# Scan attention and two feed-forward layers on one core: the second block's scores made as the first's are, an earlier place for the first block's inputs, and one PSUM bank given from the hidden products to attention

## The chip, the cores and the metric

The kernel runs on one core of one Trainium2 chip. The metric is device time of one execution in microseconds (us). The five engines of the core work on their own instruction streams and wait for each other by semaphores: TensorE (PE in the rows; its weight loads are PEld), VectorE (DVE), ScalarE (ACT), GpSimd (POOL) and SyncE (SP), which here issues every DMA. PSUM has eight banks; TensorE writes there, and VectorE and ScalarE read it.

## What is computed

First a chunked linear attention with decay over 4 batches, 8 heads, 768 positions, head size 32 and state size 16; then two feed-forward layers on the 3072 x 256 result, with 2048 hidden columns each.

```
for c in range(nc):                       # state carried from chunk to chunk
    cum = np.cumsum(log_a chunk)
    M = (Cc @ Bc.T) * exp(cum_i - cum_j) * causal
    y = M @ xc + (Cc @ state) * exp(cum)
    state = exp(sum) * state + sum_j exp(cum_last - cum_j) * Bc_j xc_j
x = y reshaped to 3072 x 256
x = elu(x @ moe_w_in) @ moe_w_out
out = mish(x @ moe2_w_in) @ moe2_w_out    # mish(h) = h * tanh(softplus(h))
```

## The kernel before

**Attention.** The kernel uses chunks of T = 96 positions. A tile is one batch at one chunk; tiles are numbered i = 4c + b, 32 in all, and the four tiles of one chunk are a block of 384 tokens. For each tile the scores (C times B, eight heads) come from TensorE into PSUM, VectorE multiplies them with the decay matrix `d` into `r` (`at_p`, L655, two products of four heads; `at_p0`, L643, four of two heads), TensorE multiplies `r` with x into `ys` (`at_y`, L677), computes the state for the next chunk (`at_st`, L709), and ScalarE and VectorE write `ys` as a high and a low part, `xyh` and `xyl` (L690, L696), the input of layer 1. `d` comes from a broadcast load of the cumulated logarithms, an addition (L536), a mask (L540) and an exponential (L545).

**Two ways to the scores.** C and B stand in memory with positions on partitions and must be transposed. Tiles in `TR0`, the first block, take the way of `at_tr0`: four fp32 transposes on TensorE into PSUM (`p_tr`, L603), one copy to SBUF (`f32t`, by ScalarE or VectorE), and eight fp32 matmuls with 16 rows each (`at_scores0`, L637), half of them per call, each half into two banks. All other tiles go through `three_parts`: C and B are split into three bf16 parts that are stacked (`stk`: two copies L506 and two L517 on ScalarE, two subtractions L511 and two L523 on VectorE or GpSimd), a DMA transpose turns the stack (L527), and eight bf16 matmuls give the scores (`at_scores`, L649), half of them per call and each half in one bank.

**Feed-forward.** A slot s is one group of 128 hidden columns of one block in one layer; 16 slots make a block of a layer, 256 slots in all, in the order of the list `order` (layer 1 of blocks 0 and 1, layer 2 of blocks 0 and 1, layer 1 of block 2, and then layer 1 and 2 in turn). TensorE makes h of a slot with six matmuls (L745 to L747: high times high, low and high parts), ScalarE and VectorE apply the activation (layer 1: L760, then L766 or L768, then L774 or L776, the last to read h; layer 2: L791 alone), split the result (`gh`, `gl`), and TensorE adds it up into `acc` some slots later (layer 1: L807 to L809; layer 2: L836 to L838; the first 16 slots do it in fp32 without a split, L812). Weights arrive in 512 KB pieces (`load_job`, L312) and each is rounded and split by `job_1` to `job_5`: L325 and L341 on VectorE, L334 on ScalarE, a copy L349 or L351, a subtraction L365 on VectorE or GpSimd.

**PSUM.** Pool `ph` (tag `h`) has HB = 4 banks: h, and the first block's scores and decay sums. Pool `pa` (tag `acc`) has 3. Pool `px` (tag `s`) has 1: transposes, the other blocks' scores and their `ys`.

**Order.** Every piece of work is a `step` with engine choices, an assumed cost and the steps that it needs. `Ring` makes a step that takes a buffer wait for those that free it. `run_steps` goes through an assumed time, gives each engine the most urgent step that is ready, and writes the instructions of each engine in that order; on the chip each engine runs its list in order. `in_turn` forces an order on some loads. No times of the chip go into it.

Of the kernel before, what the change touches and what calls it, by code (L numbers as in the profile page):

```python
# [7 lines left out]
F32 = mybir.dt.float32  # L8
# [9 lines left out]
def tile_chain(  # L18
# [13 lines left out]
    NB, H, S, D = x.shape  # L32
    N = Bm.shape[-1]
    T = 96
# [6 lines left out]
    NP = NF // FP  # L41
    LAG = 5
    N0 = NF
    TR0 = (0, 1, 2, 3)
    WB, GB, HB = 4, 3, 4

    const = ctx.enter_context(tc.tile_pool(name="const", bufs=1))
    wpool = ctx.enter_context(tc.tile_pool(name="wpool", bufs=1))
# [2 lines left out]
    gp = ctx.enter_context(tc.tile_pool(name="gp", bufs=GB))  # L51
    at = ctx.enter_context(tc.tile_pool(name="at", bufs=1))
    ph = ctx.enter_context(tc.tile_pool(name="ph", bufs=HB, space=bass.MemoryType.PSUM))
    pa = ctx.enter_context(tc.tile_pool(name="pa", bufs=3, space=bass.MemoryType.PSUM))
    px = ctx.enter_context(tc.tile_pool(name="px", bufs=1, space=bass.MemoryType.PSUM))
    dram = ctx.enter_context(tc.tile_pool(name="dram", bufs=1, space=bass.MemoryType.DRAM))

    ctx.enter_context(tc.manual_schedule())
# [5 lines left out]
    A, V, G, PE, DQ = "act", "dve", "pool", "pe", "sp"  # L64
# [9 lines left out]
    in_turn = []  # L74

    def step(opts, *deps, dl=1e9):
        steps.append((opts if isinstance(opts, list) else [opts], deps, dl))
        return len(steps) - 1
# [9 lines left out]
    class Ring:  # L88
# [5 lines left out]
        def take(self):  # L94
            self.free.append([])
            k = len(self.free) - 1
            return self.free[k], Need(self, k, self.free[k - self.n] if k >= self.n else [])

    class Need:
# [6 lines left out]
            return iter(self.free)  # L106

    rings = dict(
        w=Ring(WB), gh=Ring(GB), gl=Ring(GB), h=Ring(HB), acc=Ring(3), s=Ring(1), xy=Ring(3), x=Ring(5), bc=Ring(2),
        d=Ring(2), r=Ring(1), t=Ring(2), r1=Ring(1), bw=Ring(2), raw=Ring(2), o=Ring(3), stk=Ring(1),  # L110
    )

# [375 lines left out]
    d_t, bct, rr_t, bw_t, sp_t, s_t, ys_t, f32_t = {}, {}, {}, {}, {}, {}, {}, {}  # L488
# [109 lines left out]
    def at_tr0(i):  # L598
        p = tl["tr", i] = px.tile([112, 2, 2, T], F32, tag="s", name="p_tr")
        for z, src in enumerate((c_t[i], b_t[i])):  # L600
            for g in range(2):

                nc.tensor.transpose(  # L603
                    p[:, z, g, :], src.rearrange("p h n -> p (h n)")[:, N * g:N * g + 112], ident[0:T, 0:T]
                )

    def at_tr0_out(i, eng):
        t = f32_t[i] = gp.tile([112, 2, 2, T], F32, tag="g" + "hl"[i // 2], name="f32t")
        copy(eng, t, tl["tr", i])

    def at_diff0(i, g):
# [17 lines left out]

    def at_scores0(i, half):  # L630

        s = s_t[i, half] = [p.tile([T, 2, T], F32, tag=t, name="s") for p, t in ((ph, "h"), (pa, "acc"))]
        for g in range(2):
            for z in range(2):
                q = 32 * (2 * half + z)
                v = f32_t[i][q:q + N]
                nc.tensor.matmul(out=s[z][:, g, :], lhsT=v[:, 1, g, :], rhs=v[:, 0, g, :], start=True, stop=True)  # L637

    def at_p0(i, half):
        s, r = s_t.pop((i, half)), new_r(i)  # L640
        for z in range(2):
            hs = slice(4 * half + 2 * z, 4 * half + 2 * z + 2)
            nc.vector.tensor_tensor(out=r[0:T, hs, :], in0=s[z], in1=d_t[i][0:T, hs, :], op=ALU.mult)  # L643
# [83 lines left out]
    acc = {}  # L727
# [133 lines left out]
    def alt(f, *opts):  # L861

        return [(e, cost, lambda e=e: f(e)) for e, cost in opts]
# [4 lines left out]
    s_lc = [step((DQ, 0.48, lambda i=i: load_bc0(Cm, c_t, "xyh", i), 0.95)) for i in range(NB)]  # L868
    s_lb = [step((DQ, 0.48, lambda i=i: load_bc0(Bm, b_t, "xyl", i), 0.95)) for i in range(NB)]
# [34 lines left out]
    w_ready, LW = {}, []  # L904
    r_1, _ = take("raw")
    r_2, _ = take("raw")
# [20 lines left out]
    LX, YHI, YLO, SO, BW, xf, xy_f = {}, {}, {}, {}, {}, {}, {}  # L927
# [3 lines left out]
        LX[i] = step((DQ, 0.48, lambda i=i: load_x(i), 0.95), n)  # L931
    in_turn.append([s_la])
    for i in range(NB):
        in_turn[-1] += [s_lc[i], s_lb[i], LX[i]] + LW[i:i + 1]

    for key in [("x", 0), ("x", 1), ("y", 0), ("x", 2), ("y", 1), ("x", 3)]:
        xy_f[key] = take("xy")
# [5 lines left out]
    def three_parts(i, need):  # L943

        sf, sn = take("stk")
        rf, rn = take("r1")
        a1 = step((A, 0.82, lambda: at_split_1(i)), need, sn)
        a2 = step(alt(lambda e: at_split_2(i, e), (V, 0.40), (G, 0.45)), a1, rn)
        a3 = step((A, 0.62, lambda: at_split_3(i)), a2)
        a4 = step(alt(lambda e: at_split_4(i, e), (V, 0.40), (G, 0.45)), a3)  # L950
        tf, tn = take("t")
        a5 = step((DQ, 0.62, lambda: at_split_5(i), 2.0, True), a4, tn)
        lock.update((a2, a4))
        rf.append(a4)
        sf.append(a5)
        return a2, a5, tf

    def two_scores(i, a5, tf, ex, r_n, cold):
        pz = []
        for z in range(2):  # L960
            pf, pn = take("s")
            sc = step((PE, 0.4 if cold else 0.33, lambda z=z: at_scores(i, z)), a5, pn)
            pz.append(step((V, 0.47, lambda z=z: at_p(i, z)), sc, ex, r_n))
            pf.append(pz[-1])
            tf.append(sc)
        return pz

    for i in range(NB):
        cold = i in TR0
        if cold:  # L970
            tf, tn = take("s")
            tr = step((PE, 0.64, lambda i=i: at_tr0(i)), s_lc[i], s_lb[i], s_c2, tn)
# [4 lines left out]
        else:  # L977
            a2, a5, tf = three_parts(i, [s_lc[i], s_lb[i]])
            bc0_f.append(a2)
        if i == 0:  # L980
# [7 lines left out]
            d_f, _ = take("d")  # L988
        else:
            if i < 2:  # L990
                d_f, _ = take("d")
# [9 lines left out]
        ex = step((A, 0.78, lambda i=i: at_exp(i)), mk)  # L1001
        table[ex] = "exp"
        if i in (1, 2):
            r_f, r_n = (r_1, []) if i == 1 else (r_2, [])
        else:
            r_f, r_n = take("r")
        if cold:
            pz = []
            for z in range(2):
                hf, hn = take("h")  # L1010
                af, an = take("acc")
                sc = step((PE, 0.7, lambda i=i, z=z: at_scores0(i, z)), cp, hn, an)
# [4 lines left out]
        else:  # L1017
            pz = two_scores(i, a5, tf, ex, r_n, True)
# [23 lines left out]
    for i in range(NB, tiles):  # L1042
        c, b = divmod(i, NB)
        bcf, bcn = take("bc")
        lb = step((DQ, 0.96, lambda i=i: load_bc(i), 1.9), bcn)
        l96 = step((DQ, 1.44, lambda i=i: load_c96(i), 0.15), lb)
        d_f, d_n = take("d")
        lc = step((DQ, 0.48, lambda i=i: at_cumrow(i), 0.82), s_q4[c], d_n)
        a2, a5, tf = three_parts(i, lb)
        dd = []  # L1050
        for g in range(2):
            f = lambda e, i=i, g=g: at_diff(i, g * H // 2, (g + 1) * H // 2, e)
            dd.append(step(alt(f, (G, 1.0), (V, 0.47)), lc, s_q6))
            lock.add(dd[-1])
        mk = step((G, 0.95, lambda i=i: at_mask(i)), dd)
        ex = step((A, 0.78, lambda i=i: at_exp(i)), mk)
        table[ex] = "exp"
        cs = step((G, 0.95, lambda i=i: at_cs(i)), l96, lc, s_d5)
        r_f, r_n = take("r")
        rc = step((V, 0.56, lambda i=i: at_rc(i)), cs, r_n)  # L1060
        rc2 = step(alt(lambda e, i=i: at_rc2(i, e), (V, 0.27), (A, 0.41)), rc)
        lock.add(rc2)
        bcf += [a2, cs]
        if c + 1 < NCH:
            bf, bn = take("bw")
            b1 = step((G, 0.42, lambda i=i: at_bw_1(i)), lb, s_d3, bn)
            b2 = step((G, 0.42, lambda i=i: at_bw_2(i)), s_d7, b1)
            bcf.append(b1)
        pz = two_scores(i, a5, tf, ex, r_n, False)
        d_f += pz + [rc]  # L1070
        pf, pn = take("s")
        if c + 1 < NCH:
            y = step((PE, 0.76, lambda i=i: (at_y(i), at_st(i))), pz, rc, rc2, LX[i], pn, SO[i - NB], b1, b2)
            SO[i] = step((V, 0.34, lambda i=i: at_st_out(i)), y, LX[i + NB])
            pf.append(SO[i])
            bf.append(y)
        else:
            y = step((PE, 0.57, lambda i=i: at_y(i)), pz, rc, rc2, LX[i], pn, SO[i - NB])
        r_f.append(y)
        YHI[i] = step((A, 0.21, lambda i=i: at_y_hi(i)), y, xy_f["x", c][1])  # L1080
        YLO[i] = step((V, 0.27, lambda i=i: at_y_lo(i)), YHI[i])
        pf += [YHI[i], YLO[i]]
        xf[i].append(y)
# [3 lines left out]
    for s in range(len(order) * NF):  # L1087
        layer, c, f = at_slot(s)
        blk = s // NF
        if f == 0 and s:  # L1090
# [3 lines left out]
        h = HS[s] = step((PE, 1.95 if s < 2 else 1.04, lambda s=s: emit_h(s)), src, w_ready[f"i{layer}", f // FP], hn,  # L1094
                         HS.get(s - 1, []), dl=slot_time(s))
# [7 lines left out]
        if layer == 1:  # L1103
            e = step((A, 0.37, lambda s=s: elu_1(s)), h, wn)
            table[e] = "exp"
            e = step(alt(lambda e, s=s: elu_2(s, e), (V, 0.27), (A, 0.41)), e)
            lock.add(e)
            e = step((V, 0.47, lambda s=s: elu_3(s)), e)
        else:
            e = step((A, 0.37, lambda s=s: mish_1(s)), h, wn)  # L1110
# [3 lines left out]
        if split:  # L1114
            gf, gn = take("gh")
            lf, ln = take("gl")
            two = [(A, 0.41), (V, 0.27)]
            gh = step(alt(lambda e, s=s: split_hi(s, e), *(two if layer == 1 else two[::-1])), e, gn)
# [66 lines left out]
```

## Time and profile before

| what | us |
|---|---|
| median of 3 runs | 638.46 |
| lowest and highest | 637.58, 639.07 |
| the profiled execution | 640.66 |
| its span, first to last instruction | 638.9 |

The profiled execution lies 0.3% above the median. Of its 640.66 us the span is 638.9 us; the rest, 1.8 us, lies around it. The profile gives for each engine its busy time and, at each wait, what ended it. TensorE's busy time also holds stretches at the lower of its two clock levels.

### The profile page before, as it was taken

Reading aid. Unit: us, or ns where it says so; the run is one execution under the profiler, and the core shown is the slowest. Engines: PE = TensorE matmul, PEld = TensorE weight load, DVE = VectorE, ACT = ScalarE, POOL = GpSimd, SP = SyncE. Lnnn points to the kernel's source line nnn. Section 1 sums busy time; section 2 is a strip of 40 time slices with the busy share of each in tenths; the row PEclk is TensorE's granted clock in tenths of the full one; section 3 lists DMA queues with packets and bytes.
Section 4 is the critical chain, followed back from the end, with each engine's and each line's share of the span. In section 5 each row is a group of like instructions: output and inputs, shape, how many; then the busy total and the mean of one; then the engine's idle time right before and its main releaser. Section 6 shows DMA issues by size and latency. Waiting matters only on the chain.

```text
span 638.9 us, 12337 instructions
## 1 busy us (share of the span) xinstructions
PE 614.3 (96%) x4500; PEld 584.1 (91%) x4500; DVE 457.3 (72%) x937; ACT 402.7 (63%) x753; POOL 194.6 (30%) x259
## 2 busy tenths in 40 slices
PE   5897899998999999999999999999999999999996
PEld 4575679998999899999999999999999999999996
DVE  5688889977868887677675877668875777644443
ACT  5577888998956676548854687447855554442221
POOL 2456484453304672025600274013500210000000
PEclk9598999998999999999999999999999999999999
DMA  7789765446243552025510554024410220000000
GB/s 176 143 206 251 205 150 137 122 127 158 62 42 75 107 98 33 1 51 93 94 26 1 96 104 63 1 51 84 85 39 1 44 46 25 2 1 1 9 18 25
DMA packets 139933, 48.75 MB, mean 76 GB/s; under 512 B 122944, under 2 KB 128704, under 8 KB 139872
## 3 DMA queue, kind: packets, MB, share of 16 engines
q1 hardware_dynamic: 139872, 47.96, 35.3%
q8 instruction: 35, 0.57, 0.4%
q14 instruction: 26, 0.21, 0.1%
HBM read 32.31 MB, written 3.24 MB: 56 GB/s over the span
## 4 chain that ended last, share of the span: by engine, by line
PE 80%; DVE 7%; ACT 4%; DMA 2%; issue 2%; POOL 0%; DVEq 0%; POOLq 0%; ACTq 0%
PE h L745 13%; PE h L746 12%; PE h L747 12%; PE acc L836 7%; PE acc L838 7%; PE acc L837 7%; PE acc L807 5%; PE acc L809 5%; PE acc L808 5%; PE acc L812 3%; PE ys L709 2%; PE ys L677 2%; PE s L649 1%; DMA d<-cum_d 1%; DVE raw L341 1%
## 5 line engine op out<-in xcount | busy, mean ns | idle before, releaser
L745 PE MATMUL h<-xyh,wi 128*128 128x384 f32 x512 | 178.7, 349 | 1.7 <-ACT xyh L690 1.7
L746 PE MATMUL h<-xyl,wi 128*128 128x384 f32 x512 | 173.2, 338 | 0.1
L747 PE MATMUL h<-xyh,wi 128*128 128x384 f32 x512 | 172.8, 338 | 0.0
L787 DVE TENSOR_TENSOR gl<-w,gh 128x384 fp32r<-128x384 f32 x219 | 132.6, 609 | 17.9 <-ACT gh L349 9.0
L791 ACT ACTIVATE w<-h 128x384 f32<-128x384 f32 x128 | 61.7, 491 | 92.5 <-PE h L747 85.3
L836 PE MATMUL acc<-wo,gh 128*128 128x256 f32 x384 | 111.3, 290 | 0.0
L838 PE MATMUL acc<-wo,gl 128*128 128x256 f32 x384 | 108.5, 283 | 0.6 <-POOL gl L787 0.3
L837 PE MATMUL acc<-wo,gh 128*128 128x256 f32 x384 | 108.1, 282 | 0.0
L745 PEld LDWEIGHTS h<-xyh,wi 128*128 128x128 f32 x512 | 97.8, 191 | 4.8 <-ACT xyh L690 2.0
L746 PEld LDWEIGHTS h<-xyl,wi 128*128 128x128 f32 x512 | 97.8, 191 | 1.5 <-DVE xyl L696 0.5
L747 PEld LDWEIGHTS h<-xyh,wi 128*128 128x128 f32 x512 | 97.2, 190 | 0.2 <-DVE wi L365 0.2
L351 DVE CAST gh<-w 128x384 fp32r<-128x384 f32 x119 | 50.5, 426 | 59.5 <-PE acc L837 40.0
L760 ACT ACTIVATE w<-h 128x384 f32<-128x384 f32 x112 | 54.4, 488 | 49.7 <-PE h L747 45.2
L349 ACT ACTIVATE gh<-w 128x384 fp32r<-128x384 f32 x121 | 63.3, 523 | 31.1 <-PE acc L808 23.2
L807 PE MATMUL acc<-gh,wo 128*128 128x384 f32 x224 | 76.1, 340 | 1.1 <-DVE xyl L823 1.1
L808 PE MATMUL acc<-gh,wo 128*128 128x384 f32 x224 | 74.9, 335 | 0.0
L809 PE MATMUL acc<-gl,wo 128*128 128x384 f32 x224 | 74.9, 335 | 0.0
L838 PEld LDWEIGHTS acc<-wo,gl 128*128 128x128 f32 x384 | 72.9, 190 | 1.2 <-DVE gl L787 0.7
L836 PEld LDWEIGHTS acc<-wo,gh 128*128 128x128 f32 x384 | 72.5, 189 | 1.1
L837 PEld LDWEIGHTS acc<-wo,gh 128*128 128x128 f32 x384 | 72.7, 189 | 0.0
L768 DVE TENSOR_SCALAR w<-w 128x384 f32<-128x384 f32 x85 | 33.2, 392 | 40.2 <-ACT w L760 40.0
L536 POOL TENSOR_TENSOR d<-d,dk 96x384 f32<-96x384 f32 x39 | 35.9, 930 | 71.5 <-DMA d<-cum_d 60.5
(102 smaller groups left out, 961.7 us busy)
## 6 DMA issues: line engine op xcount, KB each, us to landing
d<-cum_d SPq DMA_DIRECT2D x31, 288.0 KB, 3.9
raw<-in_moe_w_in_dram SPq DMA_DIRECT2D x16, 512.0 KB, 5.3
raw<-in_moe_w_out_dram SPq DMA_DIRECT2D x16, 512.0 KB, 4.1
xs<-in_x_dram SPq DMA_DIRECT2D x32, 96.0 KB, 3.4
bc<-in_C_dram SPq DMA_DIRECT2D x32, 48.0 KB, 3.1
bc<-in_B_dram SPq DMA_DIRECT2D x32, 48.0 KB, 3.2
out_dram<-o SPq DMA_DIRECT2D x16, 96.0 KB, 1.8
bc<-bc SPq DMA_DIRECT2D x84, 16.0 KB, 1.8
```

Of the source, the lines that this page charges most:

```text
L349: nc.scalar.activation(out=out, in_=in_, func=AF.Copy)
L745: nc.tensor.matmul(out=h, lhsT=hi[:, k, fs], rhs=xh[:, k, :], start=(k == 0), stop=False)
L746: nc.tensor.matmul(out=h, lhsT=hi[:, k, fs], rhs=xl[:, k, :], start=False, stop=False)
L747: nc.tensor.matmul(out=h, lhsT=lo[:, k, fs], rhs=xh[:, k, :], start=False, stop=(k == 1))
L787: alu(eng).tensor_tensor(out=gl, in0=w, in1=gh.bitcast(F32), op=ALU.subtract)
L791: nc.scalar.activation(out=new_w(s), in_=st[s][0], func=AF.Mish)
L807: nc.tensor.matmul(out=y, lhsT=hi[:, f % FP, ds], rhs=gh, start=(f == 0), stop=False)
L808: nc.tensor.matmul(out=y, lhsT=lo[:, f % FP, ds], rhs=gh, start=False, stop=False)
L809: nc.tensor.matmul(out=y, lhsT=hi[:, f % FP, ds], rhs=gl, start=False, stop=(f == NF - 1))
L836: nc.tensor.matmul(out=y, lhsT=gh[:, ts], rhs=hi[:, f % FP, :], start=(f == 0), stop=False)
L837: nc.tensor.matmul(out=y, lhsT=gh[:, ts], rhs=lo[:, f % FP, :], start=False, stop=False)
L838: nc.tensor.matmul(out=y, lhsT=gl[:, ts], rhs=hi[:, f % FP, :], start=False, stop=(f == NF - 1))
```

## The change

Three edits. `TR0` becomes the first eight tiles, so that the second block (tiles 4 to 7) takes the transposing way as well; its `f32t` lies in the buffers that held the turned stack, and its scores take two `px` banks for each half. `HB` falls from 4 to 3 and `px` rises from 1 bank to 2, for the whole kernel. And the forced order of the first loads no longer has a weight load behind each tile's C, B and x: the first block's 12 loads come in a row, and the weights are free to be placed.

```
-    TR0 = (0, 1, 2, 3)
-    WB, GB, HB = 4, 3, 4
+    TR0 = range(2 * NB)
+    WB, GB, HB = 4, 3, 3
...
-    px = ctx.enter_context(tc.tile_pool(name="px", bufs=1, space=bass.MemoryType.PSUM))
+    px = ctx.enter_context(tc.tile_pool(name="px", bufs=2, space=bass.MemoryType.PSUM))
...
     def at_tr0_out(i, eng):
-        t = f32_t[i] = gp.tile([112, 2, 2, T], F32, tag="g" + "hl"[i // 2], name="f32t")
+        if i < NB:
+            t = f32_t[i] = gp.tile([112, 2, 2, T], F32, tag="g" + "hl"[i // 2], name="f32t")
+        else:
+            t = f32_t[i] = at.tile([112, 2, 2, T], F32, tag="t", name="f32t", bufs=2)
...
-        s = s_t[i, half] = [p.tile([T, 2, T], F32, tag=t, name="s") for p, t in ((ph, "h"), (pa, "acc"))]
+        banks = ((ph, "h"), (pa, "acc")) if i < NB else ((px, "s"), (px, "s"))
+        s = s_t[i, half] = [p.tile([T, 2, T], F32, tag=t, name="s") for p, t in banks]
...
-        in_turn[-1] += [s_lc[i], s_lb[i], LX[i]] + LW[i:i + 1]
+        in_turn[-1] += [s_lc[i], s_lb[i], LX[i]]
...
-        a2, a5, tf = three_parts(i, lb)
+        cold = i in TR0
+        if cold:
+            pf, pn = take("s")
+            tr = step((PE, 0.6, lambda i=i: at_tr0(i)), lb, pn)
+            tf, tn = take("t")
+            a2 = step(alt(lambda e, i=i: at_tr0_out(i, e), (A, 0.37), (V, 0.47)), tr, tn)
+            pf.append(a2)
+        else:
+            a2, a5, tf = three_parts(i, lb)
...
-        pz = two_scores(i, a5, tf, ex, r_n, False)
+        if cold:
+            pz = []
+            for z in range(2):
+                two = [take("s"), take("s")]
+                sc = step((PE, 0.65, lambda i=i, z=z: at_scores0(i, z)), a2, [n for _, n in two])
+                tf.append(sc)
+                pz.append(step((V, 0.61, lambda i=i, z=z: at_p0(i, z)), sc, ex, r_n))
+                for pf, _ in two:
+                    pf.append(pz[-1])
+        else:
+            pz = two_scores(i, a5, tf, ex, r_n, False)
```

The whole list is laid out anew, so the instructions of every engine stand elsewhere. Two places follow.

SyncE's queue from the fourth load of the program on, before the change; `bc_107` and `bc_113` are C and B of the first block, `xs` is x, `raw` a weight piece, and `d<-cum_d` the broadcast load of a tile's logarithms:

```order
L283 DMA xs<-in_x_dram 96x8x32
L312 DMA raw_118<-in_moe_w_in_dram 128x2x512
L434 DMA cum_d<-cum 16x2x96
L264 DMA bc_107<-in_C_dram 96x8x16
L264 DMA bc_113<-in_B_dram 96x8x16
L499 DMA d<-cum_d 96x768 x2
L283 DMA xs<-in_x_dram 96x8x32
L312 DMA raw_178<-in_moe_w_in_dram 128x2x512
```

And with the change, from the second tile's x on (the ninth load):

```order
L283 DMA xs<-in_x_dram 96x8x32
L264 DMA bc_107<-in_C_dram 96x8x16
L499 DMA d<-cum_d 96x768 x2
L264 DMA bc_113<-in_B_dram 96x8x16
L499 DMA d<-cum_d 96x768
L283 DMA xs<-in_x_dram 96x8x32
L264 DMA bc_107<-in_C_dram 96x8x16
L264 DMA bc_113<-in_B_dram 96x8x16
L312 DMA raw_237<-in_moe_w_in_dram 128x2x512
L283 DMA xs<-in_x_dram 96x8x32
L312 DMA raw_266<-in_moe_w_in_dram 128x2x512
```

The first weight piece moved from the 5th load to the 17th, behind C and B of all four tiles; the second stands two loads further down.

TensorE at the scores of tile 5 before the change, with buffer numbers: `s_676` and `s_692` are the two halves of the scores.

```order
L649 LDWEIGHTS t_522
L649 MATMUL s_676<-t_522 96x96
L649 LDWEIGHTS t_522
L649 MATMUL s_692<-t_522 96x96
L649 LDWEIGHTS t_522
L649 MATMUL s_692<-t_522 96x96
L649 LDWEIGHTS t_522
L649 MATMUL s_692<-t_522 96x96
L649 LDWEIGHTS t_522
L649 MATMUL s_692<-t_522 96x96
L677 MATMUL ys_705<-r_636,xs_463 32x96 x8
L709 MATMUL ys_705<-xs_463,bw_565 32x64 x4
```

The same place with the change: the accumulation of one of the first 16 slots (L816), half of the scores (L641), the six matmuls of an h, and `ys` (L681, L713).

```order
L816 MATMUL acc<-g,raw_517 128x384 x2
L641 MATMUL s<-f32t 96x96 x4
L749 MATMUL h<-xyh,wi_671 128x384
L750 MATMUL h<-xyl,wi_671 128x384
L751 MATMUL h<-xyh,wi_671 128x384
L749 MATMUL h<-xyh,wi_671 128x384
L750 MATMUL h<-xyl,wi_671 128x384
L751 MATMUL h<-xyh,wi_671 128x384
L816 MATMUL acc<-g,raw_589 128x384 x2
L681 MATMUL ys<-r,xs 32x96 x8
L713 MATMUL ys<-xs,bw 32x64 x4
```

Before, both halves and `ys` follow each other without a break. Now one h and one accumulation stand between the second half and `ys`, and another such pair stands between the two halves.

## Rows read from the trace of the kernel before

**Rows 1.** The page: busy us and share of each engine; TensorE's clock in 40 slices
```profile
PE 614.3 (96%) x4500; PEld 584.1 (91%) x4500; DVE 457.3 (72%) x937; ACT 402.7 (63%) x753; POOL 194.6 (30%) x259
...
PEclk9598999998999999999999999999999999999999
```

**Rows 2.** Windows: length, busy time of each engine (instructions), granted clock, DMA share, GB/s
```profile
0.00:14.50 14.50, 8.39 (x60) 6.73 (x60) 7.01 (x21) 7.32 (x14) 4.63 (x13) 0.97 0.73 170
14.50:30.50 16.00, 13.09 (x130) 9.20 (x131) 12.02 (x33) 9.07 (x19) 6.70 (x7) 0.50 0.76 147
30.50:55.00 24.50, 20.64 (x160) 15.84 (x159) 21.50 (x42) 19.10 (x40) 14.60 (x20) 0.99 0.94 217
55.00:58.00 3.00, 3.00 (x14) 2.83 (x13) 2.05 (x7) 2.29 (x6) 1.48 (x3) 0.50 0.82 227
58.00:95.00 37.00, 34.24 (x197) 26.19 (x197) 31.93 (x53) 30.81 (x65) 25.16 (x28) 1.00 0.78 195
95.00:190.00 95.00, 92.29 (x668) 89.98 (x669) 77.52 (x153) 81.37 (x132) 34.81 (x41) 0.98 0.44 108
240.00:639.00 399.00, 393.42 (x2877) 386.08 (x2875) 263.73 (x551) 218.38 (x407) 76.99 (x107) 1.00 0.21 40
```

**Rows 3.** Waits of TensorE over the whole span: total us, times, longest
```profile
PE s L649 <- DVE r L655: 3.6, 4, 1.8
PE ys L677 <- DVE r L655: 2.9, 3, 1.5
PE acc L812 <- DVE raw L341: 2.3, 3, 1.3
...
PE acc L807 <- DVE xyl L823: 1.1, 1, 1.1
```

**Rows 4.** Timeline to the first h: start, length, engine, line, operation
```profile
13.11 1.36 DVE L365 TENSOR_TENSOR wi<-raw,wi 128x512 fp32r<-128x512 f32 x1
...
14.91 1.33 PE L677 MATMUL ys<-r,xs 96*32 96x96 f32 x16 [1.51 <-DVE r L643]
...
23.85 1.33 PE L677 MATMUL ys<-r,xs 96*32 96x96 f32 x16 [0.72 <-DVE r L643]
...
26.50 0.31 ACT L690 ACTIVATE xyh<-ys 128x192 fp32r<-128x192 f32 x1
...
26.86 0.69 PE L745 MATMUL h<-xyh,wi 128*128 128x384 f32 x1 [1.68 <-ACT xyh L690]
```

**Rows 5.** Timelines of TensorE and VectorE around the scores of tile 5
```profile
52.43 0.34 PE L649 MATMUL s<-t 96*96 96x96 bf16 x4 [1.76 <-DVE r L655]
54.25 0.57 PE L677 MATMUL ys<-r,xs 128*32 128x96 f32 x16 [1.49 <-DVE r L655]
```

**Rows 6.** Groups by line: count, busy us, mean ns, idle us before
```profile
L506 ACT ACTIVATE stk<-bc 96x384 bf16<-96x384 f32 x56 | 26.1, 514 | 5.2 <-DMA t<-stk 3.5 <-DMA bc<-in_C_dram 1.4
...
L517 ACT ACTIVATE stk<-r 96x256 bf16<-96x256 f32 x56 | 20.2, 407 | 9.4 <-DVE r L511 7.4 <-POOL r L511 1.8
```

**Rows 7.** Timelines of TensorE at the full clock: transposing way, then bf16 way
```profile
12.32 0.61 PE L637 MATMUL s<-f32t 16*96 16x96 f32 x16 [0.51 <-ACT f32t L349]
12.86 0.54 PE L603 MATMUL p_tr<-ident,bc 96*112 96x96 f32 x4
...
61.50 0.34 PE L649 MATMUL s<-t 96*96 96x96 bf16 x4
61.68 1.53 PE L812 MATMUL acc<-g,raw 128*128 128x384 f32 x4
```

**Rows 8.** Timelines: h of slot 5, activation of slot 2; h of 53, activation of 50
```profile
37.26 0.33 PE L745 MATMUL h<-xyh,wi 128*128 128x384 f32 x1
37.53 0.54 DVE L774 SCALAR_TENSOR_TENSOR g<-g,h 128x384 f32<-128x384 f32 x1
...
162.37 0.42 PE L745 MATMUL h<-xyh,wi 128*128 128x384 f32 x1
...
164.86 0.49 ACT L791 ACTIVATE w<-h 128x384 f32<-128x384 f32 x1
```

More of the change, by code (lines that the diff above doesn't have):

```diff
@@ L108, in tile_chain @@
     rings = dict(
-        w=Ring(WB), gh=Ring(GB), gl=Ring(GB), h=Ring(HB), acc=Ring(3), s=Ring(1), xy=Ring(3), x=Ring(5), bc=Ring(2),
+        w=Ring(WB), gh=Ring(GB), gl=Ring(GB), h=Ring(HB), acc=Ring(3), s=Ring(2), xy=Ring(3), x=Ring(5), bc=Ring(2),
         d=Ring(2), r=Ring(1), t=Ring(2), r1=Ring(1), bw=Ring(2), raw=Ring(2), o=Ring(3), stk=Ring(1),
```

## The prediction, made before the changed kernel was run

> **What bounds the kernel now.** I read the page first: TensorE is busy 96% of a span of 638.9 us, and its clock line is below 9 in only three of 40 slices [rows 1]. The windows say where the rest is. From 240 us on TensorE is busy 393.42 of 399 us; nothing in this change can speed that up. The loss lies ahead: 14.50 to 30.50 us runs at a granted clock of 0.50 (the lower level, 1.2 GHz), 55 to 58 us again, and 30.50 to 55 us has TensorE busy for 20.64 of 24.50 us, with VectorE busy for 21.50 [rows 2]. The waits name who is waited for: in all the large ones it is VectorE, and most of that time falls on attention tiles [rows 3]. So this is a kernel bound by TensorE, with a start of some 27 us in which TensorE has no stream to work on, and then some 70 us in which VectorE is nearly full and TensorE is held up by single products of the attention tiles.
>
> **The change, part by part.** All changes are in us of the span.
>
> *The start.* h of slot 0 begins at 26.86, after a wait for the last tile's `xyh` [rows 4]. `ys` of tile 0 waited 1.51 for its products, and VectorE had just spent 1.36 on a weight subtraction (L365) that had been ready. `ys` of the fourth tile waited 0.72 in the same way, ended by about 25.2 (23.85 plus 1.33), and `xyh` came only at 26.50, because ScalarE was at work on splits and a weight piece. With the change the first weight piece lands behind C and B of all tiles, so that no weight work can stand ahead of tile 0 on VectorE, and the bf16 splits that stood ahead of `xyh` are gone. Upper bound: 1.51 + 0.72 + 1.0 (`xyh` at 25.5 rather than 26.50) = 3.2 saved. Lower bound: nothing, because the same weight work (L325, L341) now falls among tiles 2 and 3. I followed VectorE's new list by hand with the durations of before, and it has four L325 and L341 ahead of the fourth tile's products; that gives the first h at about 25, and I take **-1.8**. Are the weights there by then? Ahead of the first piece stand 1.64 MB of loads; at the 170 GB/s of the first window [rows 2] these and the piece of 0.51 MB take 12.7 us from about 2 us on, so it lands near 15, and its conversion (3.5 us if served at once) has until 25. I price this at nothing, with a rival below.
>
> *The second block's scores.* Gone are, for each of four tiles, two L506 and two L517 on ScalarE, 2 x 0.514 + 2 x 0.407 = 1.84, in all 7.4 us of ScalarE [rows 6]; and four DMA transposes, which SP's in-order queue held back until the stack was ready, with all loads behind them. VectorE gains little: of 16 fewer L511 and L523 it had six, it now copies `f32t` four times, and each tile has four products for two heads in place of two for four. Its list becomes some 1 us longer over the kernel. The subtractions that GpSimd loses save nothing, since GpSimd has the lowest share. TensorE pays: at the full clock both halves of a tile in fp32 take 12.86 - 12.32 = 0.54, four transposes at most 0.54, and a half in bf16 61.68 - 61.50 = 0.18 [rows 7]. That is 0.54 + 0.54 - 0.36 = 0.7 for each tile at most, 2.9 for four. The score row is 0.61 long where the next instruction begins after 0.54; with the same tail taken off the transposes it is 2.6. Tile 4's transposes and its first half stand in the start, ahead of `ys` of tile 3 or the first h, where TensorE waits in any case. So **+2.0** (bounds 1.6 and 2.9).
>
> [...] The rows on ScalarE's splits say that here the transpose is only the last of five steps.
>
> *What the waits give back.* At tile 5, TensorE waited 1.76 for the second half of the scores, then 1.49 for `ys` [rows 5], both for products that VectorE had behind a row of weight work, and then ran 55 to 58 us at the lower clock [rows 2]; there 14 matmuls took 3.00 us, and at twice the clock they would take some 1.3 less, if I leave the first one's wait in. These 3.25 + 1.3 can go, since the new order puts an h and an accumulation between the halves, and before `ys`. Of the 2.3 for L341 ahead of L812 and the 1.1 ahead of L807 [rows 3] I expect that a third goes, 1.1: weight pieces come earlier in relation to h, but VectorE is no freer. The rest of the s and `ys` waits (3.6 + 2.9 - 3.25 = 3.25) lies at later tiles, where the second `px` bank lets both halves be made at once; I take 2 of it. Against that, VectorE is the neighbour to fear: it was busy for 53.43 of the 61.5 us from 30.50 to 55 and from 58 to 95. To save 6 us there it must do the same work at 96% rather than 87%. I take off 1.4 for waits that come in new places: **-6.3** (bounds 0 and -11.2: all of these waits and the low clock).
>
> *The bank taken from h.* With three banks, h of slot s must wait until the activation of slot s-3 has read its bank. From 240 us on ScalarE is busy for 218.38 of 399 us [rows 2], so that an activation follows its h at once, and I price the bank at nothing there. Earlier it has been used: h of slot 5 begins at 37.26, before the activation of slot 2 ends at 37.53 + 0.54 = 38.07, an overlap of 0.8; h of slot 53 begins at 162.37, and the activation of slot 50 ends at 164.86 + 0.49 = 165.35, an overlap of 3.0 [rows 8]. Following the timeline between these two I found five places of this kind; with the mean of the two for each they cost 9.5 if nothing else moved, the upper bound. But where the activations set the pace, a bank more or less only shifts a wait, and ScalarE, busy for 81.37 of 95 us from 95 to 190 [rows 2], comes there with 7.4 us less behind it. I take **+0.6**, nearer to the free end, and keep 0 and 9.5.
>
> The sum: -1.8 + 2.0 - 6.3 + 0.6 = -5.5, on a span of 638.9: 633.4. The profiled execution, 640.66, lay 2.2 above the median 638.46, so the median of the changed kernel should be 638.46 - 5.5 = **633**.
>
> **The rivals.** A change of 0.2%, 1.3 us, is about what a measurement can tell.
>
> 1. *VectorE has no room* (0.18). Its work is as long as before, so 30 to 95 us shrinks by nothing, and the added matmuls lie inside waits. Only the start remains: 638.5 - 1.8 = 636.7, on the edge of no change. For it speaks VectorE's 21.50 of 24.50 us; against it, that the idle eighth of its time is there to be used, and that ScalarE, which feeds it, loses 7.4 us.
>
> 2. *The lost bank decides* (0.12): slower than before. If h stalls at all five places, 638.5 - 1.8 + 2.0 - 6.3 + 9.5 = 642. It decides from 7.4 us of stalls on, where the sum passes 639.8. For it: layer 2 of blocks 0 and 1, where ScalarE is nearly full (81.37 of 95 us) and by the code's `table` changes between weight pieces and `mish`. Against it: the order of TensorE has been laid out for three banks, with accumulations moved between h's.
>
> 3. *The weights come late* (0.06). If the first piece, moved twelve loads down, is converted only at 28, the first h comes there: 633 + 3 = 636.
>
> 4. *The transposes cost the clock* (0.05). Here the clock was low in a stretch made of such work (14.50 to 30.50), and one fall cost 1.3 (above). If each of tiles 5 to 7 brings one, and 55 to 58 stays, 633 + 4 x 1.3 = 638. The Trainium skill ("TensorE: Matmul & The Clock Gate", Part 4) says that a transpose does not count as TensorE activity. I see them between dense h streams and give it little.
>
> 5. *All waits go* (0.10), the bank is free: 638.5 - 3.2 + 1.6 - 11.2 = 626.
>
> **How the numbers follow.** The forecast, 630 to 636, has 0.49, and it is the likeliest. The range 627 to 640 leaves out most of rival 2 and the far end of rival 5, together under 0.2. Faster: the forecast, rival 5, rival 3 and half of rival 1, 0.74. Same: the other half of rival 1, rival 4, a little of rival 2, 0.15. Slower: 0.11.
>
> **What would show it.** The first h (L749) begins near 25, and the wait for `xyh` ahead of it shrinks. No wait of scores for `r` above 1 us at tiles 4 to 7, and the windows from 45 to 60 at the full clock. ScalarE's busy time down by 7 or more. TensorE waiting for L795 or L778 and L780 (the readers of h) would show the bank missing. I am wrong if the time between the first h and 95 us does not shrink, or if what is won by 95 us is given back by 190.

## The result and the profile after

| kernel | median of its runs | ratio to before | span of the profiled execution |
|---|---|---|---|
| before | 638.02 us (637.26 to 639.07, 4 runs) | 1 | 638.9 us |
| after | 631.40 us (631.16 to 632.54, 4 runs) | 0.9876 (95%: 0.9845 to 0.9908) | 630.8 us |

Faster by 1.0 to 1.2%: the ratio given is not the quotient of the two medians, which is 0.990, and its interval holds both. In medians the change saves 6.6 us, and the two profiled executions, from which all rows are taken, lie 8.1 us apart. The profiled execution of the changed kernel took 632.54 us. Its page, busy us of each engine and the clock line, answers to [rows 1]:
```profile
PE 612.7 (97%) x4548; PEld 582.9 (92%) x4548; DVE 463.8 (74%) x948; ACT 384.4 (61%) x722; POOL 198.9 (32%) x253
...
PEclk9599999999999999999999999999999999999999
```
TensorE's idle time, span less busy, went from 638.9 - 614.3 = 24.6 to 630.8 - 612.7 = 18.1 us; that is 6.5 of the 8.1 us between the profiled executions. The clock is low in the start alone. The windows answer to [rows 2]:
```profile
14.50:30.50 16.00, 12.90 (x125) 10.30 (x118) 15.73 (x34) 9.70 (x19) 9.03 (x7) 0.57 0.89 227
30.50:55.00 24.50, 22.89 (x159) 16.90 (x158) 22.46 (x46) 18.20 (x35) 12.15 (x17) 1.00 0.69 179
55.00:58.00 3.00, 3.00 (x31) 2.21 (x30) 2.99 (x8) 2.61 (x6) 1.30 (x2) 1.00 1.05 382
58.00:95.00 37.00, 35.52 (x236) 28.23 (x231) 34.80 (x65) 27.02 (x55) 24.45 (x24) 1.00 0.61 158
95.00:190.00 95.00, 93.33 (x708) 91.37 (x707) 78.78 (x149) 81.13 (x134) 42.24 (x53) 1.00 0.47 110
```
In one more stretch, from 140 to 160 us, the clock had fallen before the change. Its row before, then after:
```profile
140.00:160.00 20.00, 17.98 (x134) 17.32 (x133) 16.17 (x32) 18.23 (x28) 8.79 (x12) 0.91 0.57 152
```
```profile
140.00:160.00 20.00, 18.33 (x147) 17.49 (x146) 16.91 (x30) 19.62 (x31) 9.24 (x12) 1.00 0.56 133
```
From 55 to 58 us TensorE now runs 31 matmuls at the full clock, where it had run 14 at half of it. VectorE is busy for 34.80 of 37 us from 58 to 95, where it had been for 31.93: it does find the room that rival 1 denied it. The waits of TensorE over the whole span, total, times and longest, answer to [rows 3]:
```profile
PE p_cr L620 <- DVE cum L422: 4.2, 1, 4.2
PE ys L681 <- DVE r L647: 2.7, 4, 0.9
PE h L749 <- DVE w L780: 1.5, 1, 1.5
PE h L749 <- ACT w L795: 1.3, 2, 1.1
PE acc L816 <- DVE raw L341: 0.9, 1, 0.9
PE acc L816 <- DVE g L780: 0.8, 1, 0.8
PE p_tr L603 <- DMA bc<-in_C_dram: 0.7, 1, 0.7
PE acc L841 <- DVE wo L365: 0.4, 1, 0.4
```
No score and no `ys` of the attention tiles waits for `r` any more once the h stream runs; the four `ys` waits that are left lie in the start. The two h rows are new: h waits for its readers to give a bank back. The two longest of these waits:
```profile
89.13 0.44 PE L749 MATMUL h<-xyh,wi 128*128 128x384 f32 x1 [1.47 <-DVE w L780]
```
```profile
157.97 0.44 PE L749 MATMUL h<-xyh,wi 128*128 128x384 f32 x1 [1.07 <-ACT w L795]
```
The start, which answers to [rows 4]:
```profile
13.05 1.15 PE L681 MATMUL ys<-r,xs 96*32 96x96 f32 x16 [0.35 <-DVE r L647]
...
21.61 0.89 PE L603 MATMUL p_tr<-ident,bc 96*112 96x96 f32 x4 [0.72 <-DMA bc<-in_C_dram]
23.42 1.06 PE L681 MATMUL ys<-r,xs 96*32 96x96 f32 x16 [0.92 <-DVE r L647]
24.41 0.96 PE L641 MATMUL s<-f32t 16*96 16x96 f32 x8
25.30 0.69 PE L749 MATMUL h<-xyh,wi 128*128 128x384 f32 x1
```
The first `ys` comes 1.86 us earlier and waits 0.35 in place of 1.51; the first h comes at 25.30 in place of 26.86, and without its wait for `xyh`.

Where the gain arises, from the start of a slot's first h in the two timelines: it is 1.6 us at slot 0, 3.6 at slot 20 (88.0 to 84.4), 3.5 at slot 36 (122.2 to 118.7), 6.2 at slot 64 (193.02 to 186.86), 8.3 at slot 112 (309.1 to 300.8) and 8.4 at slot 255 (626.2 to 617.8). Less than half of it is made in the first 95 us. Single slots scatter, since each order puts the other work elsewhere between them: slot 40 gives 1.1 and slot 50 gives 8.7.

### The profile page after: what moved, and what is told of

It reads as the page before. It is cut to its first block, busy times and chain, and to the rows that moved or that the text cites. A ratio compares the mean times of both kernels' runs of the same rounds, so it can differ in the third digit from the quotient of the medians.

```text
span 630.8 us, 12397 instructions
## 1 busy us (share of the span) xinstructions
PE 612.7 (97%) x4548; PEld 582.9 (92%) x4548; DVE 463.8 (74%) x948; ACT 384.4 (61%) x722; POOL 198.9 (32%) x253
## 4 chain that ended last, share of the span: by engine, by line
PE 74%; DMA 8%; DVE 7%; issue 4%; ACT 3%; SPq 3%; POOL 1%; DVEq 0%; POOLq 0%
PE h L749 11%; PE h L750 11%; PE h L751 11%; PE acc L840 6%; PE acc L811 6%; PE acc L813 6%; PE acc L812 6%; PE acc L842 6%; PE acc L841 6%; DMA raw<-in_moe_w_out_dram 2%; DMA raw<-in_moe_w_in_dram 1%; PE ys L681 1%; DMA d<-cum_d 1%; DVE raw L341 1%; DMA cum_d<-cum 1%
## 5 line engine op out<-in xcount | busy, mean ns | idle before, releaser
L791 DVE TENSOR_TENSOR gl<-w,gh 128x384 fp32r<-128x384 f32 x214 | 129.2, 606 | 18.5 <-ACT gh L349 9.1
L349 ACT ACTIVATE gh<-w 128x384 fp32r<-128x384 f32 x118 | 61.8, 524 | 33.5 <-PE acc L812 23.5
L791 POOL TENSOR_TENSOR gl<-w,gh 128x384 fp32r<-128x384 f32 x26 | 29.4, 1132 | 149.2 <-PE s L653 108.7
L812 PE MATMUL acc<-gh,wo 128*128 128x384 f32 x224 | 74.8, 334 | 0.0
L772 DVE TENSOR_SCALAR w<-w 128x384 f32<-128x384 f32 x92 | 37.7, 411 | 37.6 <-ACT w L764 36.9
```

The lines of the kernel that those rows point to most:

```text
L349: nc.scalar.activation(out=out, in_=in_, func=AF.Copy)
L791: alu(eng).tensor_tensor(out=gl, in0=w, in1=gh.bitcast(F32), op=ALU.subtract)
L812: nc.tensor.matmul(out=y, lhsT=lo[:, f % FP, ds], rhs=gh, start=False, stop=False)
```

## The experiments

All were timed in five rounds. The first four shared their runs of the kernel before (median 640.19 us), as did the next four (640.34) and the last four (640.31); the ratios go by these. The medians of before differ by up to 2.3 us from the 638.02 of the result, so kernels are compared by their ratios. The ratios differ by up to 0.15% from the quotients of the medians. The loads, the banks and the transposes are the three parts of the change.

**e1, the loads alone:** of the diff only this line.
```diff
-        in_turn[-1] += [s_lc[i], s_lb[i], LX[i]] + LW[i:i + 1]
+        in_turn[-1] += [s_lc[i], s_lb[i], LX[i]]
```


> The kernel before with the edit of the forced load order alone. My theory: the start is worth its own term only, first h near 25.3 as with the whole change, time 636.4 (1.6 less than before), waits of scores for products at tiles 4 to 7 still there. Rival, all of the gain comes from the loads: 631.5. Rival, the gain is luck of a new layout: anything from 630 to 640, with the first h not moved.

649.63 us (647.66 to 651.74), 1.0140 (1.0115 to 1.0164): slower, where 636.4 was expected. TensorE's waits and its clock line:
```profile
PE ys L677 <- DVE r L655: 6.1, 4, 2.8
...
PE acc L812 <- DVE raw L341: 3.3, 2, 2.1
PE h L745 <- DVE wi L351: 2.5, 1, 2.5
```
```profile
PEclk9599799997999999999999999999999999999999
```
The first h came at 25.5, as expected, but behind it `ys` waits 6.1 for `r` in place of 2.9 (the scores 1.1 in place of 3.6), new waits for weights stand beside it, and two of the 40 slices behind the start are well below full clock.

**e2, the banks alone:** `HB` 3, two `px` banks, `s=Ring(2)`.

> The kernel before with the PSUM bank moved alone (h 3 banks, px 2), second block by the bf16 way. My theory: the waits of scores and ys for products shrink by 2 to 4 us, the missing h bank costs about 1, time 635.5; first h unmoved at 26.9. Rival, the lost bank decides: 640 or more, with TensorE waiting for the readers of h. Rival, luck of layout: no relation.

640.34 us, 1.0000 (0.9982 to 1.0018), where 635.5 was expected. No h waits for its readers, so the lost bank is not what ate the gain, though the time is the rival's. The waits of scores and `ys` for `r` fell from 6.5 us to 0.8, and others took their place, among them:
```profile
PE h L745 <- DVE wi L351: 2.4, 1, 2.4
PE h L747 <- DVE wi L365: 2.3, 2, 1.6
PE s L649 <- DMA t<-stk: 2.1, 1, 2.1
```

**e3, the transposes alone:** with one `px` bank a half can't have two banks, so the scores go in four pieces of two heads.
```diff
-    TR0 = (0, 1, 2, 3)
+    TR0 = range(2 * NB)
...
+            for k in range(4):
+                pf, pn = take("s")
+                sc = step((PE, 0.33, lambda i=i, k=k: at_scores_q(i, k // 2, k % 2)), a2, pn)
```


> The kernel before with the second block by TensorE transposes alone: banks as before, so the scores of tiles 4 to 7 are made in four pieces of two heads, each in the one px bank. My theory: ScalarE is freed of 7.4 us, but the one bank keeps TensorE waiting for each product, so 637, between no change and 3 us faster. Rival, lighter ScalarE alone is what brings the gain: 632. Rival, transposes only cost TensorE time: 640.

642.66 us, 1.0033 (1.0019 to 1.0047), where 637 was expected. TensorE idles 7.1 us less than before and is busy 8.7 us longer: the waits went, and the work ate more than they gave.

**e4, the lost bank alone:** the order of before to the last instruction, with three h banks.
```diff
-    ph = ctx.enter_context(tc.tile_pool(name="ph", bufs=HB, space=bass.MemoryType.PSUM))
+    ph = ctx.enter_context(tc.tile_pool(name="ph", bufs=3, space=bass.MemoryType.PSUM))
```


> The kernel before, its instruction lists unchanged, but the pool of h has 3 banks and one bank lies unused. This prices the bank with nothing else moved; bounds of the prediction 0 and 9.5. My theory: overlaps of 0.8 to 3.0 at five places, partly absorbed, +3 us, 641, with waits of TensorE for the readers of h (L774, L776, L791) at slots 5 to 7, 32, 40 and 53. Rival, the activations set the pace there and the bank is free: 638, no such waits. Rival, it is worth the full 9.5: 647.

652.2 us, 1.0191 (1.0165 to 1.0217). The waits of h for its readers:
```profile
PE h L745 <- ACT w L791: 5.1, 5, 2.3
...
PE h L745 <- DVE g L774: 3.5, 3, 1.6
...
PE h L745 <- DVE w L774: 0.7, 1, 0.7
PE h L745 <- DVE w L776: 0.3, 1, 0.3
```
They make 9.6 us, near the 9.5 of the prediction's upper bound for an order in which nothing moves, and far above the 3 expected here. That the two agree so well is luck: the bound was five places of 1.9 each, and these are ten waits of 1.0 in the mean. By the medians the time grew by 12.0 us, more than the waits of the profiled execution, which was the fastest of its six. The changed kernel's order was laid out for three banks and pays 1.5 + 1.3 = 2.8.

The parts alone gave +1.4%, 0 and +0.3%, and together -1.2%: they don't add. The second set took them in pairs, against three theories: that transposes and second `px` bank are one edit (A), that the early loads need SP's queue free of the second block's transposes (B), and that each new order scatters the time by itself (C).

**e5, loads and banks.**

> Loads moved and the bank moved, the second block's scores as before. In the first four runs the parts alone gave 1.014 (loads), 1.000 (banks) and 1.003 (transposes) of before, together some 11 us slower, and all three at once 8 us faster: the sum of parts fell. Theory A (the score path): the transposes and the second px bank are one edit, and without the transposes the early loads stay harmful, because the five steps of the scores on ScalarE and VectorE meet earlier weight work: about 648 against 639 of before, ratio 1.01 to 1.02. Theory B (the queue): the moved loads and the bank have little to do with each other, so e1 and e2 add: 1.014. Theory C (the layout): the written-out order is re-planned for every edit and scatters by some us whatever the edit is; any ratio between 0.99 and 1.02, with its extra time in single waits at other places than those of e1. Told apart from A and B by the places: A wants ys and s waiting for r of tiles 4 to 7.

636.52 us, 0.9944 (0.9925 to 0.9964): neither A nor B as stated; C allows it.

**e6, transposes and banks:** the changed kernel with the loads of before.

> The changed kernel but with the loads in the order of before. Theory A: this is the pair that carries the gain; only the start is as before, so 631.4 + 1.6 = 633, ratio 0.990 to 0.993. Theory B (the early loads carry the gain, and only harm where SP's queue still has transposes of the second block in it): about 640, ratio 1.00. Theory C: anything between 0.99 and 1.02.

634.39 us, 0.9908 (0.9888 to 0.9928): as A has it; B falls. C, which allows anything from 0.99 to 1.02, allows this too.

**e7, loads and transposes, one px bank.**

> Loads moved and the transposes, but four h banks and one px bank, in which the scores go in four pieces of two heads. Theory A: the pieces stand in line for one bank, so tiles 4 to 7 wait as in e3, and the early weight work is still there: 640 to 645, ratio 1.00 to 1.01. Theory B: the queue is free of the second block's transposes, so the loads' gain is there: 634 or less, ratio 0.99. Theory C: anything between 0.99 and 1.02.

643.57 us, 1.0052 (1.0031 to 1.0073): as A has it, and again as C allows.

**e8, the third block too:** `TR0 = range(3 * NB)`.

> The changed kernel with the third block's four tiles scored from transposes too. Theory A: ScalarE loses another 4 x 1.84 = 7.4 us in the stretch from 95 to 240 us, TensorE gains 2 to 2.9 us of work, and TensorE has few waits left there that could pay for it (2 to 3 us): 632 to 634 against 631.4. Theory C: 628 to 640, with the difference in single waits.

635.43 us, 0.9925 (0.9905 to 0.9945): by the ratios 0.5% slower than the changed kernel, with intervals that just meet, and within what a new order by itself can do (e10 to e12). TensorE is busy 4.5 us longer (617.2), its idle time is 0.8 shorter (17.3): there was little left to give back.

**e9, the order of a half's products:** the changed kernel with its order kept, but the two products of a pair of row groups one behind the other.
```diff
-        for g in range(2):
-            for z in range(2):
+        for g, z in ((0, 0), (0, 1), (1, 0), (1, 1)) if i < NB else ((0, 0), (1, 0), (0, 1), (1, 1)):
```


> The changed kernel with its order of instructions kept, but in each half of the second block's scores the two products of one pair of row groups follow each other, where the changed kernel alternates between the two pairs. In e3 and e7, which had one bank for these products and so could not alternate, the group took 9.6 and 10.0 us for 32 products (64 records), against 8.2 - 3.6 = 4.6 in the changed kernel. Theory (the alternation runs two products side by side, and this is a part of what the second px bank buys): of the four products of a half only the middle two still overlap, some 0.30 more for each of eight halves, the group 2 to 2.6 us longer, the time 633 to 634, ratio 0.991 to 0.992. Rival (e3 and e7 lost by the stop after each piece, not by the row groups): the group stays at about 8.2 and the time at 631.4, ratio 0.988.

632.63 us, 0.9887 (0.9868 to 0.9907), and a half is as long as before. So the alternation is not it. The rows of halves and pieces themselves show what is: a half in e9, then in the changed kernel, then a piece in e3, each with the row behind it (start, length).
```profile
50.77 0.59 PE L640 MATMUL s<-f32t 16*96 16x96 f32 x8
51.29 0.45 PE L748 MATMUL h<-xyh,wi 128*128 128x384 f32 x1
```
```profile
51.40 0.58 PE L641 MATMUL s<-f32t 16*96 16x96 f32 x8
51.91 0.44 PE L749 MATMUL h<-xyh,wi 128*128 128x384 f32 x1
```
```profile
67.75 0.57 PE L648 MATMUL s<-f32t 16*96 16x96 f32 x4
68.25 0.45 PE L761 MATMUL h<-xyh,wi 128*128 128x384 f32 x1
```
A piece of 4 records (one row group), a half of 8 (two) and both halves of a first-block tile, 16 (four, [rows 7]), take 0.57, 0.58 and 0.61; each fp32 product shows as two records. A fixed price for each piece would read the same, but the starts of the single records tell the two apart. In e3's piece they come one at a time (67.910, 67.996, 68.081), in the changed kernel's half in pairs some 6 ns apart (51.560 and 51.566, 51.645 and 51.651). So what stands in different row groups runs side by side, and a tile costs TensorE some 0.5 for each piece that it is cut into. The one bank of e3 and e7 cuts it into four, and 16 pieces at 0.50 cost 3.9 us more than 8 halves at 0.51. They are busy 9 to 12 us longer than the changed kernel and e6. Part of the rest is a fallen clock, 0.91 from 60 to 100 us in e3 and 0.87 from 30 to 60 in e7, which at twice the clock gives some 4 us in each.

**e10, before with another order:** nothing but one estimate of the planner is changed, for the mask, by 1%.
```diff
-        mk = step((G, 0.95, lambda i=i: at_mask(i)), dd)
+        mk = step((G, 0.96, lambda i=i: at_mask(i)), dd)
```


> The kernel before with nothing changed but one estimate of the planner, the mask's 0.95 to 0.96, which writes out another order of the same instructions. Theory (the layout's scatter is small, the parts of the edit decide): within 0.4% of before. Rival (the layout scatters as much as the edits move): off by 0.5 to 2%, either way. With it the edit's parts could not be told from their layouts in single runs.

646.25 us, 1.0101 (1.0081 to 1.0121). The same work in another order, with some steps on other engines (VectorE has 954 instructions in place of 937), and 1% slower: the rival's case.

**e11, the changed kernel with the same other estimate.**

> The changed kernel with the mask's estimate 0.95 to 0.96 and so another order. Theory (the parts decide): 630 to 634, ratio 0.985 to 0.993, TensorE's idle time 17 to 20 us as in all four kernels with the transposes. Rival (layout): 635 to 645.

637.25 us, 0.9951 (0.9935 to 0.9967): in time this is the rival's case, and the ratio lies just outside the theory's. The idle time, 20.9, lies just above the theory's 17 to 20.

**e12, e1 with the same other estimate.**

> e1 (the loads alone) with the mask's estimate 0.95 to 0.96; the order is e1's up to the second block's tiles and another one behind them. Theory (early weight loads by themselves do harm): 646 to 652, ratio 1.01 to 1.02, as e1. Rival (e1's 9 us were its layout's): 634 to 643, ratio 0.99 to 1.005.

642.64 us, 1.0050 (1.0031 to 1.0069), at the edge of the rival's range: most of e1's loss was its layout's. Behind the start its longest waits now stand at L812, 5.8 us.

**All of them side by side.** Idle is the span less TensorE's busy time, of the profiled execution.

| kernel | loads | banks | transposes | ratio | busy | idle | first h at |
|---|---|---|---|---|---|---|---|
| before | | | | 1 | 614.3 | 24.6 | 26.9 |
| e10, before, other order | | | | 1.0101 | 615.4 | 28.0 | 25.5 |
| e4, order of before | | h bank only | | 1.0191 | 613.4 | 34.6 | 26.2 |
| e2 | | yes | | 1.0000 | 612.3 | 24.8 | 25.9 |
| e1 | yes | | | 1.0140 | 618.3 | 30.8 | 25.5 |
| e12, e1, other order | yes | | | 1.0050 | 613.3 | 27.6 | 23.9 |
| e5 | yes | yes | | 0.9944 | 611.4 | 22.6 | 24.3 |
| e3 | | | yes, in pieces | 1.0033 | 623.0 | 17.5 | 25.5 |
| e7 | yes | | yes, in pieces | 1.0052 | 624.6 | 18.7 | 25.3 |
| e6 | | yes | yes | 0.9908 | 613.8 | 18.7 | 27.7 |
| after | yes | yes | yes | 0.9876 | 612.7 | 18.1 | 25.3 |
| e9, after, products swapped | yes | yes | yes | 0.9887 | 612.4 | 18.2 | 25.1 |
| e11, after, other order | yes | yes | yes | 0.9951 | 615.1 | 20.9 | 24.0 |
| e8, three blocks | yes | yes | yes | 0.9925 | 617.2 | 17.3 | 25.6 |

Three things can be read from it in spite of the scatter. With the transposes TensorE idles for 17.3 to 20.9 us, without them for 22.6 to 34.6, in seven kernels each (e9 has the order of the changed kernel, e4 that of before). With transposes and one bank it is busy for 623.0 and 624.6, with two banks for 612.4 to 617.2. And the first h begins at 23.9 to 25.6 with the loads moved (mean 24.9), at 25.5 to 27.7 without (mean 26.3); in all five pairs that differ in the loads alone it is earlier with them moved, by 0.2 to 2.4. As a whole the change gave 0.9876 in the one order and 0.9951 / 1.0101 = 0.985 in the other.

## Why the prediction was right

633 was forecast, 631.40 measured, inside the range, and the likeliest case came. The mechanism is the one that was foreseen: the waits for `r` in the h stream went, against some more work on TensorE. But the sum was nearer than its terms, and that is luck: two costs were set too low, by 3.4 together, and one gain by 5.1.

- **The start, -1.8:** -1.56, as followed by hand. VectorE had three L325 and two L341 rows ahead of the fourth tile's products, near the four foreseen. The table gives the loads 1.4 us in the mean, but a new order without them does as much (e10 against before), so of this one 1.56 their part isn't shown. Weights were not late there (rival 3): the first h waited for nothing.
- **Extra work, +2.0 (at most 2.9): mis-sized.** A tile's first and second half were priced together at 0.54. That is right where both are issued at once, in the first block's four banks; in two `px` banks the halves stand apart and cost 0.51 each. From start to next start: seven halves in the h stream 7 x 0.51 = 3.6, three sets of transposes at 0.32, 0.33 and 0.38 (not 0.54) = 1.0, less the eight bf16 halves that stood there, 8 x 0.18 = 1.4: +3.2. The Trainium skill ("TensorE: Matmul & The Clock Gate", Part 3) says that products in different row groups overlap; the 0.57, 0.58 and 0.61 agree. Read beside [rows 7], it would have warned that half a tile need not be half the price.
- **Waits and clock, -6.3: mis-sized; -11.4, past its own bound of -11.2.** After the first h the waits of [rows 3] with the smaller ones for `gl` (0.3 and 0.2) came to 10.4; of them 0.9 + 0.8 + 0.4 = 2.1 are left or new, h apart: -8.3. Both waits at tile 5 are gone, as are the later ones of s and `ys`, of which only 2 of 3.25 were taken, and L807's. The clock no longer falls at 55 us (the 1.3 foreseen) nor near 150, where 95 to 190 us had 0.98 and has 1.00: the fall there was left out of the sum. 20 us from 140 on had 0.91 before, at twice the clock 0.09 x 20 = 1.8 us less.
- **The bank, +0.6 (at most 9.5): mis-sized in an order planned for it,** 2.8, and for the reason given: h of one slot at 89.13 waits 1.47 for VectorE, one at 157.97 waits 1.07 for ScalarE. Not all of it need be the bank's, since orders planned for four banks wait for L791 as well (1.0 in e10, 1.8 in e12). The bound, 9.5, was met by e4's waits, 9.6, in another way than foreseen, and passed by its time. That the planner could avoid most of it is shown by e6, whose h waits for neither reader.
- **The sum** of these, -1.6 + 3.2 - 8.3 - 1.3 - 1.8 + 2.8 = -7.0, leaves 1.1 of the 8.1 us unplaced.
- **ScalarE, 7 or more:** 18.3. L506 and L517 make 26.1 - 22.3 + 20.2 - 17.2 = 6.8 of it; six loads of tables fewer at 1.28 make 7.7, and the rest is the planner's new sharing of work.
- **VectorE, "some 1 us longer":** 6.5 (457.3 to 463.8). The second block had ten of the 16 subtractions on VectorE and six on GpSimd, not the other way round. Against that the planner gave VectorE other work, and its 32 L325, the same number as before, took 21.5 us in place of 16.9; what made them longer stays open.
- **The stretch:** the gain was sought ahead of 95 us. It is there: of the 3.6 at slot 20, 2.1 arose behind the first h, where 3.5 of waits and 1.3 of the low clock went against the 3.2 of extra work. The larger part of the whole came behind 122. "Given back by 190" did not happen.
- **The rivals.** 1 fell with VectorE's 34.80 of 37 us. 4 fell: transposes at 45.08 and 58.40 lie in windows at a clock of 1.00. 2 is what e4 is: without a new order the bank alone would have decided. Of 5, the waits and the low clock went as it says, but the bank wasn't free and the work cost twice its 1.6.

What the prediction didn't see is that any edit of this kernel draws a new order, and that a new order by itself moved the time by +1.0% (e10 against before), +0.8% (e11 against after: 0.9951 / 0.9876) and -0.9% (e12 against e1). By the medians these are 0.9, 0.6 and -1.1%. The whole change is no larger than that, so its one time alone shows little. That the transposes with their bank are at work in it is shown by the idle column and by e6, e8, e9 and e11, all faster than before. How much of the 8 us is theirs and how much the order's luck stays open: e5, without the transposes, reaches 0.9944 and is level with e11. Open too is what the loads or the banks are worth alone: e1 and e12, which are both the loads alone, lie 0.9% apart, and e6, which lacks the loads, can't be told from the changed kernel (0.9888 to 0.9928 against 0.9845 to 0.9908). No version tried beats the changed kernel clearly, and e9 equals it.

## What to carry to other kernels

Where a planner writes out the order, run one pure re-plan (an estimate moved by 1%) beside the edit, before a part of it is credited with less than 1%; TensorE's idle and busy time, read over several orders, tell more than single times, though each order moves them too (idle 24.6 and 28.0 for the kernel before). A buffer moved from one use to another must be priced under the order that is planned for it: the same lost bank cost 9.6 us of waits in the old order and 0 to 2.8 in new ones. Small products in separate row groups should be issued together: what a tile costs goes by the number of pieces, and so by the banks that are free at once.

## What was not expected of the hardware

4, 8 and 16 fp32 matmul records of 16 rows took 0.57, 0.58 and 0.61 us when they lay in one, two and four row groups; with the two groups of a half issued one behind the other the half took 0.59 (e9). Records of different groups started some 6 ns apart, those of one group some 85 ns apart.
